# Position bias as a small relu layer, x transposed on TensorE, v loaded once, more buffers of p

## The chip, the cores and the metric

The kernel runs on one core of a Trainium2 chip. The metric is the device time of one execution in microseconds (us), lower is better. Engines are TensorE (PE; its weight loads are PEld), VectorE (DVE), ScalarE (ACT), GpSimd (POOL) and SyncE (SP), with 16 DMA engines beside them. SP and ACT issue DMAs from queues of their own.

## The reference

Attention with a bias that depends on positions, then two mixing blocks. B = 4 batches, H = 8 heads, S = 576 positions, D = 64, hidden layer of 32. In short:

```python
scores = q @ k.T / 8
x = log1p(abs(i - j)) / log1p(max(i, 1))          # S x S
bias = relu(x[..., None] @ w1 + b1) @ w2          # S x S x H, the same for all batches
attn = softmax(scores + bias)
x = (attn @ v), heads side by side                # B x S x 512
# block 1: h = gelu(x @ w_in); u, v = halves of h; layer norm of v; v_s = w_sg @ v + b_sg
x = x + (u * v_s) @ w_out
# block 2: theta = x @ w_theta; y = w_tok_r @ (x cos theta) + w_tok_i @ (x sin theta)
u = x + y;  out = u + relu(u @ w_ch)
```

## The kernel before

The program records every operation with its operands, and a planner in `Rec.plan` (a list scheduler) decides on the order in which each engine gets them. It has a price for every operation (`cost`), a due time (`nc.key`, moved by the table `SHIFT`), a choice of engine for operations with alternatives (`BIAS`), and knows when buffers come free. Buffers are taken from tags with a fixed number of copies, and the copies of one tag are handed out in the order of the program text. Every instruction is emitted from one helper line (L377), so groups are told apart by the names of their tiles.

The stages, in the order of the text of `build`:

- `bias_gen`. The bias for all heads is built in SBUF, in `bm[0..3]` (128 query rows each, 8 heads, 576 columns) and `bm[4]` (the last 64 rows, two heads on the two halves of the partitions). A relu unit is on where a distance lies above a threshold, so for 45 blocks VectorE compares a table of distances `ds` with thresholds `th` into `mk` (128x2048 f16, rows are 4 columns times 32 units), TensorE multiplies `mk` by `w2*w1` and by `w2*b1`, each in two f16 parts `ch` and `cl` (1440 products of 64 columns), ScalarE copies one half out (`cc`), VectorE multiplies the other by x (`bt`; for some blocks GpSimd does it from a copy `ca`), and GpSimd adds the two into the bias. Beside it ScalarE squares all of v (`vr`) for a scale.
- `att_pair`, for 4 batches and 4 pairs of heads. `prep` loads k and q (`kq`) and v (`raw`, 128x1152 f32: all of v's rows in nine blocks of 128, the list of rows being v twice) and makes f16 parts `v16`. A pair has nine tiles: four blocks of 128 queries for each head, and the last 64 queries of both heads in one tile. Per tile (`att_tile`): scores by f32 products, bias added and the row's extreme found in one VectorE operation (`e`), Exp on ScalarE, p in two f16 parts (the high one on ScalarE as a rule, the low one on GpSimd), one transposing DMA from SP's queue into `pT` (nine blocks of 128x128), and products of `pT` with `v16` into `px`, one PSUM tile that all pairs share.
- The pair's result is divided by the row sums (`pair_main`, `pair_rem`), cut into two f16 parts (`x16`), transposed by a DMA into `xp`, and stored in DRAM (`dx`).
- `mlp(b)`: the first half of block 1 for batch b. It loads `xT` from `dx` and runs 15 units of f16 products (`vp`, `up`, `sp`), each into a PSUM tile of tag `c` (three copies), and stores its result to `dg`. In the program text mlp(b) stands behind the pairs of batch b and ahead of those of b+1; its due time lies well inside batch b+1.
- The tail: conversion of f64 weights, `s2` (the second half of block 1, which reads x again from `dx` as `xx` and adds its two parts on GpSimd), `theta`, `ymix` and `s4` (block 2).

Of the kernel before, what the change touches and what calls it, by code (L numbers as in the profile page):

```python
# [26 lines left out]
NP = H // 2  # L27
# [32 lines left out]
class V:  # L60
# [3 lines left out]
    def __getitem__(self, idx):  # L64
# [3 lines left out]
        for k, n in enumerate(self.shape):  # L68
# [4 lines left out]
            if d is not None:  # L73
                o = box[d][0]
                box[d] = (o + lo, o + hi)
# [119 lines left out]
def lap(a, b):  # L195
    return all(x[0] < y[1] and y[0] < x[1] for x, y in zip(a, b))


def covers(a, b):
    return all(x[0] <= y[0] and y[1] <= x[1] for x, y in zip(a, b))  # L200
# [3 lines left out]
    ("bsg", "scalar"): -41.5201, ("bsg", "sync"): -39.1168, ("g", "scalar"): -6.4798, ("g", "sync"): -12.4768,  # L204
    ("gg", "gpsimd"): -53.3129, ("gg", "scalar"): 53.8735, ("gg", "sync"): -40.1577, ("gg", "vector"): 12.8746,
    ("gr", "scalar"): 40.0426, ("gr", "sync"): -7.2604, ("ident", "scalar"): 17.1516,
    ("ident", "sync"): 113.1953, ("kq", "scalar"): -21.5876, ("kq", "sync"): -29.2704, ("m", "gpsimd"): -0.0246,
    ("m", "vector"): -0.3984, ("n", "gpsimd"): 35.1559, ("n", "scalar"): -32.6866, ("n", "vector"): -2.2379,
    ("oo", "scalar"): -24.802, ("oo", "sync"): 41.6395, ("p", "gpsimd"): -12.0341, ("p", "scalar"): 0.77,
    ("p", "vector"): 2.7135, ("raw", "scalar"): -44.0014, ("raw", "sync"): 28.1704,  # L210
    ("raww_ch", "scalar"): -43.3259, ("raww_ch", "sync"): 25.28, ("raww_out", "scalar"): 10.1527,
    ("raww_out", "sync"): -7.508, ("raww_theta", "scalar"): -30.2437, ("raww_theta", "sync"): 36.9561,
    ("raww_tok", "scalar"): -80.3857, ("raww_tok", "sync"): -15.2151, ("rawwi", "scalar"): 13.2129,
    ("rawwi", "sync"): 14.8861, ("ri", "gpsimd"): -15.2269, ("ri", "vector"): 3.6268,
# [4 lines left out]
    ("wr_w_ch", "gpsimd"): 3.5242, ("wr_w_ch", "vector"): 6.6705, ("wr_w_out", "gpsimd"): 21.1998,  # L219
    ("wr_w_out", "vector"): -58.3817, ("wr_w_theta", "gpsimd"): -22.3734, ("wr_w_theta", "vector"): -49.8466,  # L220
    ("wr_w_tok", "gpsimd"): -17.5048, ("wr_w_tok", "vector"): -57.1214, ("ws", "scalar"): -34.0239,
    ("ws", "vector"): 34.9878, ("wsr", "scalar"): 49.7733, ("wsr", "vector"): 31.3292,
# [5 lines left out]
}  # L228
SHIFT = {
# [355 lines left out]


T0, TS = 88.0, 2.35
TWO = range(4,45,6)
PBN = (0,0,1)
T2 = T0 + TS * 144  # L590

# [761 lines left out]
```

## Time and profile before

| | before |
|---|---|
| runs, median (lowest to highest) | 920.55 us (917.52 to 922.99), 3 runs |
| the profiled execution: time | 922.0 us |
| the profiled execution: span from the first to the last instruction | 920.2 us |
| mean granted TensorE clock | 0.894 |
| busy: PE, DVE, ACT, POOL | 81%, 72%, 57%, 46% of the span |

Busy time is the time in which an engine has an instruction under way. Products overlap, so that a busy TensorE need not be at its peak. The granted clock is a share of 2.4 GHz. A group of instructions is named by what it writes and reads, as `pT<-p`; what ended an engine's idle time stands behind it with an arrow.

### The profile page before, as it was taken

Reading aid. Unit: us, or ns where it says so; the run is one execution under the profiler, and the core shown is the slowest. Engines: PE = TensorE matmul, PEld = TensorE weight load, DVE = VectorE, ACT = ScalarE, POOL = GpSimd, SP = SyncE. Lnnn points to the kernel's source line nnn. Section 1 sums busy time; section 2 is a strip of 40 time slices with the busy share of each in tenths; the row PEclk is TensorE's granted clock in tenths of the full one; section 3 lists DMA queues with packets and bytes.
Section 4 is the critical chain, followed back from the end, with each engine's and each line's share of the span. In section 5 each row is a group of like instructions: output and inputs, shape, how many; then the busy total and the mean of one; then the engine's idle time right before and its main releaser. Section 6 shows DMA issues by size and latency. Waiting matters only on the chain. (4 is left out here: it accounts for less than half of the span.)

```text
span 920.2 us, 19119 instructions
## 1 busy us (share of the span) xinstructions
PE 742.5 (81%) x7322; PEld 558.2 (61%) x7322; DVE 660.5 (72%) x1391; ACT 525.5 (57%) x1064; POOL 421.0 (46%) x363
## 2 busy tenths in 40 slices
PE   3555356757769878789897989999878999999998
PEld 3554343544544444455455545567767999989998
DVE  8989975799787865477764776989999782472712
ACT  6432247888777865567865764756666651261600
POOL 3777685555655645465654653333244521140400
PEclk9768776875788988899998899999889999999999
DMA  8300029999999999999899877355631100010001
GB/s 290 102 1 1 1 77 208 179 201 202 221 218 198 198 174 165 202 188 190 181 197 219 143 144 246 113 179 159 210 114 35 47 31 21 14 39 1 34 19 52
DMA packets 221307, 120.04 MB, mean 130 GB/s; under 512 B 195104, under 2 KB 195232, under 8 KB 221216
## 3 DMA queue, kind: packets, MB, share of 16 engines
q1 hardware_dynamic: 215360, 104.40, 51.7%
q10 hardware_dynamic: 5856, 14.42, 6.2%
q8 instruction: 57, 0.93, 0.4%
q14 instruction: 34, 0.28, 0.1%
HBM read 57.45 MB, written 14.16 MB: 78 GB/s over the span
## 5 line engine op out<-in xcount | busy, mean ns | idle before, releaser
L377 POOL TENSOR_TENSOR p<-e,p 128x576 f16<-128x576 f32 x144 | 189.1, 1322 | 127.7 <-ACT p L377 84.2
L377 PEld LDWEIGHTS <-pT 128*128 128x128 f16 (+1 forms) x2240 | 87.1, 108 | 114.3 <-DMA pT<-p 66.5
L377 PE MATMUL px<-v,pT 128*128 128x64 f16 (+1 forms) x2240 | 100.3, 204 | 64.8 <-DMA pT<-p 55.2
L377 PE MATMUL s<-kq 64*128 64x288 f32 (+1 forms) x640 | 138.1, 508 | 15.9 <-DVE m L377 10.1
L377 DVE CUSTOM_DVE_ANT_0 e<-s,bias 128x576 f32<-128x576 f32 x128 | 95.7, 752 | 62.6 <-PE s L377 47.6
L377 ACT ACTIVATE e<-e,m 128x576 f32<-128x576 f32 x144 | 110.2, 766 | 49.2 <-DVE m L377 35.4
L377 PE MATMUL yp<-wk,z 128*128 128x288 f32 x864 | 117.3, 296 | 0.0
L377 ACT ACTIVATE p<-e 128x576 f16<-128x576 f32 x142 | 94.1, 671 | 40.2 <-DMA pT<-p 38.0
L377 PEld LDWEIGHTS yp<-wk,z 128*128 128x128 f32 x864 | 115.3, 188 | 0.4
L377 PE MATMUL pb<-ch,mk 128*128 128x64 f16 x720 | 60.8, 214 | 58.2 <-ACT cc L377 33.9
L377 PEld LDWEIGHTS s<-kq 64*128 64x128 f32 (+1 forms) x640 | 71.4, 212 | 54.4 <-DVE m L377 22.1
L377 PEld LDWEIGHTS <-mk 128*128 128x128 f16 x1440 | 59.1, 112 | 60.6 <-DVE mk L377 46.0
L377 DVE TENSOR_TENSOR mk<-ds,th 128x2048 f16<-128x2048 f16 x45 | 80.4, 1831 | 5.4 <-PE pb L377 5.4
L377 POOL TENSOR_TENSOR bias<-bt,cc 128x512 f32<-128x512 f32 x36 | 63.6, 1789 | 34.3 <-ACT cc L377 34.3
L377 PE MATMUL op<-sp_g,wo 128*128 128x288 f32 x384 | 61.9, 320 | 14.1 <-DVE x L377 12.8
L377 PEld LDWEIGHTS op<-sp_g,wo 128*128 128x128 f32 x384 | 57.2, 206 | 19.0 <-issue 10.6
L377 ACT ACTIVATE cc<-pb,ci 128x512 f32<-128x512 f32 x45 | 29.5, 685 | 64.2 <-DVE bt L377 62.2
L377 PE MATMUL vp<-wi,xT 128*128 128x512 f16 (+1 forms) x240 | 64.9, 408 | 0.8 <-DMA xT<-dx 0.8
L377 PE MATMUL sp<-ws,n 128*128 128x64 f16 (+1 forms) x384 | 58.8, 293 | 3.6 <-DVE n L377 3.1
L377 PE MATMUL pb<-cl,mk 128*128 128x64 f16 x720 | 60.7, 214 | 0.0
L377 PE MATMUL up<-xT,wi 128*128 128x64 f16 (+1 forms) x384 | 57.8, 297 | 0.0
L377 DVE TENSOR_TENSOR x<-x,yp 128x576 f32<-128x576 f32 x16 | 12.0, 753 | 62.8 <-PE yp L377 62.8
(217 smaller groups left out, 1381.7 us busy)
## 6 DMA issues: line engine op xcount, KB each, us to landing
kq<-kq SPq DMA_DIRECT2D x13, 576.0 KB, 5.4
raw<-vp SPq DMA_DIRECT2D x10, 576.0 KB, 4.9
raww_tok<-w_tok SPq DMA_DIRECT2D x18, 288.0 KB, 3.1
vr<-v_all SPq DMA_DIRECT2D x12, 384.0 KB, 4.1
xx<-dx SPq DMA_DIRECT2D x16, 288.0 KB, 3.4
out<-oo SPq DMA_DIRECT2D x16, 288.0 KB, 2.1
gr<-dg SPq DMA_DIRECT2D x14, 288.0 KB, 3.3
dg<-gg SPq DMA_DIRECT2D x14, 256.0 KB, 3.0
```

What stands on the lines that cost most here:

```text
L377: getattr(getattr(self.nc, name), m)(*[res(x) for x in a], **out)
```

## The change

The bias: one hidden unit of one query row is relu(w1/psi_i * log1p|i-j| + b1). A table `lt` holds log1p of distances for 32 units times 4 rows that lie 8 apart; a window of it, times a per-partition `sl`, gives the hidden layer of four query rows as one 128x576 f32 tile `hq`. There are 36 groups G of four such tiles. Two groups of three make them on VectorE, as max(window*sl, -b1), to which a constant per head is added back at the end; every third on ScalarE, as Relu with scale and bias. Eight f32 products multiply them by w2 (128 rows to 32 outputs: 4 rows times 8 heads), with the four tiles of a group going to partitions 0, 32, 64 and 96 of the same PSUM tile. One evacuation makes `bs`, and a DMA copies its 128 rows to bias rows 8 apart (for the last 64 query rows four smaller DMAs). `mk`, `bt`, `cc`, `ca` and the tables for them go.

x: the pair's f32 result is transposed on TensorE (`flip`: four transposes of 128x128, and one of 64x128) into a PSUM tile of tag `c`, and both f16 parts are made from there into `xT`, which stays in SBUF (six copies, one per pair) and is stored to `dx` for the tail. mlp reads it in SBUF.

v: the first five blocks are loaded, and the other four are copied on VectorE between the two halves of the partitions. p16 has six copies instead of four, pT eight instead of four. The planner's constants (`BIAS`, `SHIFT`, yields, some prices) have other values throughout.

```diff
@@ bias_gen
-        for n in range(45):
...
-                nc.vector.tensor_tensor(mk, win, th[:, ib * P:(ib + 1) * P].bc(1, 16), op=ALU.is_gt)
...
-            for J in range(16):
...
-                nc.tensor.matmul(o, mk[:, J, :], chv, start=True, stop=False)
-                nc.tensor.matmul(o, mk[:, J, :], clv, start=False, stop=True)
...
-            nc.scalar.activation(cc, pv[:, H:], AF.Copy, scale=ci8)
...
-                self.tt(("gpsimd",), dv, tmp[r, :nh], cc[r, hs], ALU.add)
+        for G in range(36):
...
+            lut = G % LUTG == LUTG - 1
+            for q in range(4):
...
+                h = st.tile([P, S], F32, tag="hq", bufs=10, name=f"hq{Q}")
+                win = lt[:, DOFF - i0:DOFF - i0 + S]
+                if lut:
+                    nc.scalar.activation(h, win, AF.Relu, scale=sl[:, Q:Q + 1], bias=b1)
+                else:
+                    nc.vector.tensor_scalar(h, win, sl[:, Q:Q + 1], nb, op0=ALU.mult, op1=ALU.max)
+                hs.append(h)
+            for n in range(2):
+                for q in range(4):
+                    nc.tensor.matmul(ps[32 * q:32 * q + 32, n, :SH], w2f, hs[q][:, n * SH:(n + 1) * SH],
+                                     start=True, stop=True)
...
+            nc.any(("scalar", "activation", (bv, ps[:, :, :SH], AF.Identity), {"bias": add}),
+                   ("vector", "tensor_scalar", (bv, ps[:, :, :SH], add, None), {"op0": ALU.add}))
             if ib < 4:
+                self.ld(self.bm[ib][c:P:8], bs)
             else:
+                for k in range(2):
+                    for e in range(2):
+                        self.ld(self.bm[4][64 * e + c + k:64 * e + 64:8], bs[64 * k + e:64 * k + 64:2])
@@ prep
-        raw = a.tile([P, 2, S], F32, tag="raw", bufs=1, name=f"raw{u}")
+        raw = a.tile([P, 2, 5 * D], F32, tag="raw", bufs=1, name=f"raw{u}")
...
-        self.cp(v16[:, 0], vr, self.sv)
+        self.cp(v16[:, 0, :, 0:5], vr, self.sv)
+        nc.vector.tensor_copy(v16[0:64, 0, :, 5:9], v16[64:P, 0, :, 0:4])
+        nc.vector.tensor_copy(v16[64:P, 0, :, 5:9], v16[0:64, 0, :, 1:5])
@@ att_tile
-        p16 = a.tile([P, 2, S], F16, tag="p16", bufs=4, name=f"p{u}")
+        p16 = a.tile([P, 2, S], F16, tag="p16", bufs=6, name=f"p{u}")
-        pT = a.tile([P, 9, P], F16, tag="pT", bufs=4, name=f"pT{u}")
+        pT = a.tile([P, 9, P], F16, tag="pT", bufs=8, name=f"pT{u}")
@@ pair_main, pair_rem
-        self.cp(x16[:, :4, 0], xf)
-        self.tt(("gpsimd", "vector"), x16[:, :4, 1], xf, x16[:, :4, 0], ALU.subtract)
+        self.flip(p, u, xf, xT, 0, 4)
+
+    def flip(self, p, u, xf, xT, o, n):
+        nc = self.nc
+        m = xf.shape[0]
+        w = m * n
+        pt = self.cps(f"xq{u}")
+        for t in range(n):
+            nc.tensor.transpose(pt[:, t * m:(t + 1) * m], xf[:, t] if n > 1 else xf, self.ident[:m, :m])
+        self.cp(xT[:, 0, o:o + w], pt[:, :w])
+        nc.vector.tensor_tensor(xT[:, 1, o:o + w], pt[:, :w], xT[:, 0, o:o + w], op=ALU.subtract)
@@ att_pair
-        x16 = a.tile([P, 5, 2, P], F16, tag="x16", name=f"x16_{b}_{p}")
-        xp = a.tile([P, 2 * S], F16, tag="xp", bufs=1, name=f"xp{b}_{p}")
+        xT = self.xT[b, p] = self.p_x.tile([P, 2, S], F16, tag="xT", bufs=6, name=f"xT{b}_{p}")
...
-        nc.sync.dma_start_transpose(out=xp.rearrange("p (t k) -> p t k", k=P),
-                                    in_=x16.rearrange("p t s k -> p (t s k)")[:, 0:1152])
-        self.ld(self.dx[b, :, p], xp)
+        self.ld(self.dx[b, :, p], xT.rearrange("p s t -> p (s t)"))
@@ mlp
-        self.xT = self.p_x.tile([P, 4, 2 * S], F16, tag="xT", name=f"xT{b}")
-        for p in range(0, NP, 2):
-            self.ld(self.xT[:, p:p + 2], self.dx[b, :, p:p + 2])
@@ s2
+            nc.gpsimd.tensor_tensor(xs, xx[:, :S], xx[:, S:], op=ALU.add)
```

## Rows read from the trace of the kernel before

**Rows 1.** The page's head.

```profile
span 920.2 us, 19119 instructions
```

**Rows 2.** Three stages: us, busy us (instructions) by engine, granted clock, DMA, GB/s.

```profile
0.00:138.00 138.00, 68.35 (x1460) 63.11 (x1460) 118.08 (x147) 53.58 (x92) 91.36 (x68) 0.79 0.23 79
138.00:548.00 410.00, 328.79 (x3488) 195.64 (x3487) 296.19 (x811) 298.88 (x642) 225.44 (x204) 0.85 1.00 192
548.00:920.00 372.00, 345.32 (x2375) 299.48 (x2375) 246.27 (x434) 173.10 (x331) 104.19 (x92) 0.98 0.26 81
```

**Rows 3.** Groups of 0 to 134 us: busy us, mean ns, idle before.

```profile
L377 DVE TENSOR_TENSOR mk<-ds,th 128x2048 f16<-128x2048 f16 x45 | 80.4, 1831 | 5.4 <-PE pb L377 5.4
L377 POOL TENSOR_TENSOR bias<-bt,cc 128x512 f32<-128x512 f32 x36 | 63.6, 1789 | 34.3 <-ACT cc L377 34.3
L377 PE MATMUL pb<-ch,mk 128*128 128x64 f16 x720 | 60.8, 214 | 58.2 <-ACT cc L377 33.9 <-DVE mk L377 18.8 <-DVE bt L377 5.5
...
L377 ACT ACTIVATE cc<-pb,ci 128x512 f32<-128x512 f32 x45 | 29.5, 685 | 64.2 <-DVE bt L377 62.2 <-PE pb L377 1.7
```

**Rows 4.** SP's queue from 515 us: start, us, what it issued.

```profile
524.85 14.72 SPq L377 DMA_TRANSPOSE pT<-p  x8
```

**Rows 5.** DMA issues: count, KB each, median us to landing.

```profile
xT<-dx ACTq DMA_DIRECT2D x5, 576.0 KB, 6.7
...
pT<-p SPq DMA_TRANSPOSE x144, 4.0
...
xp<-x SPq DMA_TRANSPOSE x16, 4.2
```

**Rows 6.** Waits of the engines, whole span: us in total, times, longest.

```profile
PEld L377 <- DMA pT<-p: 66.5, 36, 5.6
...
PE px L377 <- DMA pT<-p: 55.2, 30, 5.0
...
ACT p L377 <- DMA pT<-p: 38.0, 16, 5.2
```

**Rows 7.** Waits of SP's queue, 138 to 548 us.

```profile
SPq L377 <- POOL p L377: 103.9, 73, 4.2
```

**Rows 8.** The table prow in the start: ns min/median/max, first and last start.

```profile
L377 DVE TENSOR_SCALAR prow<-prow,rt x1: 520/520/520, 6.4 to 6.4; 128x576 f32<-128x576 f32 x1
L377 DVE TENSOR_SCALAR prow<-prow x1: 460/460/460, 7.0 to 7.0; 128x576 f32<-128x576 f32 x1
```

**Rows 9.** The tile xt.

```profile
L377 ACT ACTIVATE xt<-xt,ci x5: 758/774/777, 8.9 to 11.9; 128x576 f32<-128x576 f32 x5
```

**Rows 10.** The tile vr.

```profile
L377 ACT ACTIVATE vr<-vr x12: 827/843/844, 6.5 to 35.9; 128x768 f32<-128x768 f32 x12
```

**Rows 11.** The PSUM tile xp of the tail.

```profile
L377 DVE TENSOR_TENSOR rk<-xp,rk x18: 672/684/692, 676.1 to 872.8; 128x512 f32<-128x512 f32 x16, 64x512 f32<-64x512 f32 x2
```

**Rows 12.** TensorE in order of time, at 220 and at 313 us.

```profile
220.25 2.85 PE L377 MATMUL s<-kq 64*128 64x288 f32 x8
...
313.39 1.24 PE L377 MATMUL s<-kq 64*128 64x288 f32 x8
314.57 0.58 PE L377 MATMUL px<-v,pT 128*128 128x64 f16 x14
```

**Rows 13.** The tile s of the scores.

```profile
L377 PE MATMUL s<-kq x640: 402/403/846, 126.8 to 533.3; 64*128 64x288 f32 x128, 64*64 64x288 f32 x32
```

**Rows 14.** The chain that ended last: start, us, what.

```profile
756.79 0.66 PE xp L377 x4
```

**Rows 15.** The tile v.

```profile
L377 ACT ACTIVATE v<-raw,fc_v x16: 1238/1248/1256, 129.3 to 511.6; 128x1152 f16<-128x1152 f32 x16
```

**Rows 16.** The page's costliest groups: the products of the MLP.

```profile
L377 PE MATMUL vp<-wi,xT 128*128 128x512 f16 (+1 forms) x240 | 64.9, 408 | 0.8 <-DMA xT<-dx 0.8
...
L377 PE MATMUL sp<-ws,n 128*128 128x64 f16 (+1 forms) x384 | 58.8, 293 | 3.6 <-DVE n L377 3.1
...
L377 PE MATMUL up<-xT,wi 128*128 128x64 f16 (+1 forms) x384 | 57.8, 297 | 0.0
```

More of the change, by code (lines that the diff above doesn't have):

```diff
@@ L195, in lap @@
 def lap(a, b):
-    return all(x[0] < y[1] and y[0] < x[1] for x, y in zip(a, b))
+    return all(x[0] < y[1] and y[0] < x[1] and not (x[2:] and x[2:] == y[2:] and (x[0] - y[0]) % x[2])
+               for x, y in zip(a, b))
 def covers(a, b):
-    return all(x[0] <= y[0] and y[1] <= x[1] for x, y in zip(a, b))
+    return all(x == y or (not x[2:] and x[0] <= y[0] and y[1] <= x[1]) for x, y in zip(a, b))
 BIAS = {
-    ("bsg", "scalar"): -41.5201, ("bsg", "sync"): -39.1168, ("g", "scalar"): -6.4798, ("g", "sync"): -12.4768,
@@ L205 @@
[L205 to L209, printed above, removed]
@@ L587 @@
 T0, TS = 88.0, 2.35
-TWO = range(4,45,6)
-PBN = (0,0,1)
+LUTG = 3
 T2 = T0 + TS * 144
@@ L704, in bias_gen @@
-        self.th = nc.vector.tensor_scalar(th, y2, 0.5, sg2, op0=ALU.add, op1=ALU.mult)
-        nc.vector.tensor_scalar(ds, ds, sg2, None, op0=ALU.mult)
-        c32 = st.tile([P, 2, H, 4], F32, name="c32")
-        nc.vector.memset(c32, 0.0)
+        sl = st.tile([P, S // 4], F32, name="sl")
+        lt = st.tile([P, DW], F32, name="lt")
+        for x, n in ((wb, "wb"), (sl, "rpsi"), (lt, "ltab")):
+            self.ld(x, d[n])
+        nb = st.tile([P, 1], F32, name="nb")
+        nc.vector.tensor_scalar(nb, b1, -1.0, None, op0=ALU.mult)
@@ L708, in bias_gen @@
+        self.th = nc.vector.tensor_scalar(sl, sl, w1, None, op0=ALU.mult)
+        w2s = st.tile([P, 4, H], F32, name="w2s")
+        nc.vector.memset(w2s, 0.0)
         for g in range(4):
             r = slice(32 * g, 32 * g + 32)
-            nc.vector.tensor_scalar(c32[r, 0, :, g], w2[r], w1[r], None, op0=ALU.mult)
-            nc.vector.tensor_scalar(c32[r, 1, :, g], w2[r], b1[r], None, op0=ALU.mult)
-        c32f = c32.rearrange("p a h g -> p (a h g)")
-        junk = self.bsg[:, :64]
-        for i in range(2):
-            nc.scalar.activation(junk, c32f, AF.Square, accum_out=self.ss_c[:, i:i + 1])
@@ L725, in bias_gen @@
-        for n in range(45):
-            nc.key = 2.0 * n
-            ib, js = divmod(n, 9)
-            if js == 0:
-                nc.any(("scalar", "activation", (xt[:, ib], xt[:, ib], AF.Copy), {"scale": ci8}),
-                       ("vector", "tensor_scalar", (xt[:, ib], xt[:, ib], ci8, None), {"op0": ALU.mult}))
-            mk = st.tile([P, 16, P], F16, tag="mk", bufs=3, name=f"mk{ib}_{js}")
-            off = DOFF + ib * P - js * 64
+            nc.vector.tensor_scalar(w2s[r, g], w2[r], 8.0, None, op0=ALU.mult)
@@ new lines, in bias_gen @@
+        w2f = w2s.rearrange("p g h -> p (g h)")
+        cb = st.tile([P, 1], F32, name="cb")
+        bb = st.tile([P, 1], F32, name="bb")
+        pc = self.ps_b.tile([P, 2, 512], F32, tag="pb", bufs=2, name="pbc")[:, 0]
+        nc.vector.tensor_copy(bb, b1)
+        for g in range(4):
+            nc.tensor.matmul(pc[32 * g:32 * g + 32, 0:1], w2f, bb, start=True, stop=True)
+        nc.vector.tensor_copy(cb, pc[:, 0:1])
+        zero = st.tile([P, 1], F32, name="zb")
+        nc.vector.memset(zero, 0.0)
@@ L1308, in layout @@
     a["wb"] = np.tile(w, (4, 1))
-    pos = np.arange(S)
-    pi = np.log1p(np.maximum(pos.astype(f), f(1.0)))
-    a["prow"] = np.tile(pi[None], (P, 1))
-    a["dtab"] = np.abs(np.arange(DW)[None] - DOFF - (np.arange(P) // HID)[:, None]).astype(np.float16)
-    rel = np.log1p(np.abs((pos[:, None] - pos[None]).astype(f)))
-    x = (rel / pi[:, None]).astype(f)
-    x = np.concatenate([x, x[512:]], axis=0)
-    a["xtab"] = x.reshape(5, P, S).transpose(1, 0, 2)
+    psi = np.log1p(np.maximum(np.arange(S).astype(f), f(1.0)))
+    rows = [[G // 8 * P + G % 8 + 32 * q if G < 32 else 512 + 2 * (G - 32) + 32 * (q % 2) + q // 2 for q in range(4)]
+            for G in range(36)]
+    rows = np.array(rows).reshape(1, S // 4) + 8 * np.arange(4)[:, None]
+    a["rpsi"] = np.repeat(f(1.0) / psi[rows], HID, axis=0)
+    a["ltab"] = np.log1p(np.abs(np.arange(DW)[None] - DOFF - 8 * (np.arange(P) // HID)[:, None]).astype(f))
     a["ident"] = np.eye(P, dtype=f)
```

188 lines of the change are left out of this document (65 added, 123 removed), and 33 rows, old and new, of tables (BIAS, SHIFT).

## Prediction

> **What bounds the kernel now.** I read the page's head and its 40 slices first, then busy time by stage, then each stage's own groups, prices, queue and waits. The profiled execution has a span of 920.2 us and a time of 922.0; the median of the runs shown is 920.55, so what holds for the profile holds for the median less 1.5 us [rows 1]. Cut at the first transposing DMA of p (138 us) and behind the last products with p (548 us), the kernel has three stages [rows 2]. In the start (138 us) the DMA engines work 0.23 of the time, and VectorE 118 of 138 us. In the attention (410 us) no engine is above 329 of 410, but the DMA share is 1.00. In the tail (372 us) TensorE is busy 345 us at a granted clock of 0.98, and the chain that ended last lies there, on its matmuls.
>
> The start makes the bias. VectorE's 45 comparisons that write mk take 80 us, GpSimd's adds into bias 64, TensorE's two products with mk 61 each, and TensorE waits for mk and for cc [rows 3]. It is a cycle of four engines at VectorE's pace.
>
> In the attention each tile's p goes through one transposing DMA. Eight of them issued back to back by SP take 14.72 us, 1.84 each, where nothing but the DMA engines holds the queue [rows 4]. 160 of them (144 of p, 16 of x; a tile of 128x1152 f16, 0.295 MB) [rows 5] make 294 us of the 410. The rest, 116 us, is for ordinary copies: 192 GB/s times 410 us [rows 2] is 78.7 MB, less 160 x 0.295 MB, so 31.5 MB at 3.7 us per MB. TensorE and ScalarE wait for pT: 66.5 us before weight loads, 55.2 before products, 38.0 before p is written [rows 6]. Against a pure DMA bound speaks in the same stretch that SP itself waits 103.9 us for GpSimd's half of p [rows 7]: the producers are not far ahead.
>
> **The start, part by part.** Removed: mk, the 1440 products, bt, cc and GpSimd's adds. Added: 144 relu tiles of 128x576 f32, 96 on VectorE and 48 on ScalarE (every third group of four rows' tiles); 288 f32 products of 288 columns with 32 rows of output; 36 evacuations; 48 copies of bias rows (10.6 MB).
> - VectorE: a 128x576 tensor_scalar takes 0.46 us with constants and 0.52 with one per-partition operand [rows 8]; the new one has two. Lower bound 0.52, upper one step of 0.06 more; I take 0.58: 96 x 0.58 = 56 us.
> - ScalarE: 0.774 with one per-partition operand [rows 9]; two, by a like step, 0.87: 48 x 0.87 = 42 us. The 12 squares of v stay, 0.84 each [rows 10], 10 us.
> - Evacuations go to either engine: cc's 128x512 took 0.685 on ScalarE [rows 3], an operation reading 128x512 from PSUM 0.684 on VectorE [rows 11]; for 576 columns about 0.76: 36 x 0.76 = 27 us.
> - Sum 135 us on two engines, 68 each if shared evenly. Work starts at about 9 us (before, the first products start at 11), so the relu work ends at 77; the first transpose of p came 4 us behind the first attention tile, and I add 2 for uneven sharing: 83 us instead of 138, **-55**.
> - TensorE must stay under those 68 us. An f32 product of 288 columns is two passes, and the scores show eight passes, two at a time on the two halves of the rows, in 1.24 us at full clock [rows 12], each recorded as 0.40 to its end [rows 13]. Four steps with the last one whole: (1.24 - 0.40)/3 = 0.28 a step, the first with its weight load in it; I take 0.25, a product 0.50. 288 products, four side by side, are 36 us; two by two 72; one after another 144. Side by side in columns is not in this trace, only in rows; the scores overlap fully, so I take 36 to 72, hidden behind the 68 or nearly. The Trainium skill (TensorE: Matmul & The Clock Gate, Part 3: packing small matmuls) gives 2.38 times for three column tiles; by that 58 us, an estimate, also hidden.
> - Copies: the start now moves 138 us x 79 GB/s = 10.9 MB [rows 2]; with 10.6 more and 1.5 of table less, 20 MB at 3.7 us per MB is 74 us, under the 83. The cover is thin: at 4.2 us per MB the copies would set the end. The 3.7 was measured beside the transposes, which the start has none of, so I leave the copies at nothing; at twice the price they would add 65.
>
> **The attention.** The 16 transposes of x go: 16 x 1.84 = 29 us of DMA. v is read as 640 f32 columns instead of 1152, 256 KB less each, 15 times in this stage (3.9 MB), and the reads of xT for three batches go, 6 x 576 KB (3.5 MB) [rows 5]: 7.4 MB x 3.7 = 27 us. So the DMA work falls by 56, from 410 to 354. The Trainium skill (Advanced Engine Details and Errata, X-Bar Transpose) expects 350 to 400 GB/s of a transposing DMA; one of 295 KB would take 0.8 us, an estimate, the 16 be worth 13, and the fall be 40. The eight in 14.72 us contradict it.
>
> What takes the place: TensorE gets five small transposes per pair; four f32 ones of 128x128 take 0.66 us [rows 14], so with the fifth about 0.9, 14 us in all, and its 329 become 343 at the clock then granted. VectorE has x's subtraction now from PSUM, 0.68 by the nearest row [rows 11], where it was from SBUF, and gets two copies of 64x512 f16 per pair, bounded by the 0.46 above and by nothing: 0 to 15 us on 296. ScalarE converts 640 instead of 1152 columns, 1.248 us now [rows 15], about 7 us less in all. None reaches 354, but all stand at 83 to 97% of it.
>
> There is also a new order. The flip's PSUM block comes from the tag that the MLP uses, three buffers handed out in the program's order, and mlp(b) stands ahead of the pairs of batch b+1. So flip(b+1, 0) waits until mlp(b) is nearly through; xf and xfr have one buffer each, so the next pair's px can't be emptied, and attention stops some 16 tiles into batch b+1. Behind it wait the products with p, then pT (8 buffers), then SP's transposes. mlp(b) needs 65, 58 and 59 us by four [rows 16], 45 us of TensorE. The 16 tiles need half of 1.24 for scores and at most 0.58 for px each [rows 12], 19 us. Together 64, against (16 + 8) x 354/144 = 59 us of cover. Lower bound of the price nothing; upper bound, with the MLP alone in all three batches but for the eight buffered tiles, 3 x (45 - 20) = 75. The need is nearest to the cover, so I take a stall of 5 per batch and some refilling, 20 us in all: 354 + 20 = 374, **-36**. p and pT with 6 and 8 buffers I cost at nothing by themselves; they are in this cover.
>
> **The tail.** x's way through DRAM to the last mlp goes, but TensorE is busy 345 of 372 us there [rows 2]: **-3**, between 0 and -15 where mlp(2) moves ahead of the attention's end. xs by one GpSimd add instead of two is off the path. The planner's other constants only reorder; I give them no sign.
>
> **Sum.** 922.0 - 55 - 36 - 3 = 828 by the profile's time, 827 by the median.
>
> **Rivals.**
> 1. *The attention keeps its length.* SP's 104 us of waiting for GpSimd speak for it, and the new order; the waits for pT against. 922 - 55 - 3 = 864, with the upper bound of the stall (354 + 75 = 429) 883.
> 2. *Column groups don't overlap, at full clock.* 144 us of products instead of 68: start 9 + 144 + 6 = 159, +21; 922 + 21 - 36 - 3 = 904. For it only that the trace has no such case.
> 3. *Slower than before.* The same, at the lower level of the clock. The start's granted clock is 0.79 now [rows 2], between the levels of 1.2 and 2.4 GHz; at the lower one the eight passes took 2.85 us instead of 1.24 [rows 12], so a product is 1.0. Start 9 + 288 + 6 = 303, +165: 1048. It decides once a product costs more than (138 + 39 - 15)/288 = 0.56 us, a price between those of the two levels. Against it: in the tail, where TensorE has hardly a gap, 0.98 was granted [rows 2].
> 4. *All of the DMA's relief shows, and mlp(2) leaves the tail.* 922 - 55 - 56 - 15 = 796.
>
> **Chances.** Forecast 0.55, with its own range 805 to 850; rival 1 0.22; rival 2 0.07; rival 3 0.05; rival 4 0.09; a change that nets out to nothing 0.02. The range 785 to 890 takes in rival 4, rival 1 with its bound, and leaves out rivals 2 and 3 and a little. A measurement of this kernel tells about 0.5% from no change: faster 0.93, same 0.02, slower 0.05.
>
> **What the profile after would show.** The first transpose of p at 75 to 95 us; VectorE and ScalarE both above 0.8 in the start; four hq products starting within a few tens of ns of each other (if 0.24 us apart, rivals 2 or 3); 144 transposes, none of x; attention of 355 to 390 us with waits for pT shorter, and stalls, if any, where a batch begins, with the flip's block behind the MLP. I am wrong if the start is bound by the copies or TensorE, or if p is late at GpSimd as often as before.

## The result, and the profile after

| | before | after |
|---|---|---|
| median (lowest to highest) | 921.77 us (917.52 to 927.09), 4 runs | 884.49 us (881.56 to 889.14), 4 runs |
| profiled execution: time, span | 922.0, 920.2 us | 881.6, 879.8 us |
| mean granted TensorE clock | 0.894 | 0.917 |

The ratio is 0.960 [0.953, 0.967]: 37 us faster. The forecast's sum had 94 us. More than half of that gain did not come, and the rest of this text is about where it went.

The page of the changed kernel, its head, its busy times and three of its rows of 40 slices:

```profile
span 879.8 us, 17586 instructions
...
PE 762.3 (87%) x6544; PEld 534.8 (61%) x6544; DVE 629.9 (72%) x1475; ACT 520.5 (59%) x1038; POOL 298.4 (34%) x263
...
PE   5689778648899889997999976998878999999998
...
PEclk9979956557999999999799996999999999999999
DMA  7987689729898299866998396465622210010101
```

The head answers to [rows 1]. TensorE is busier than before (762 us against 742) in a shorter span, the DMA engines are no longer full in the middle, and the clock row has one hole, in slices 6 to 10 (110 to 220 us).

For the stages, the first cut of [rows 2] (the first transpose of p) no longer parts anything, since the first pair's attention now runs beside the bias: its first transpose is issued at 53 us. So both kernels are cut at the tenth transpose of p (the second pair's first tile) and at the end of the products with p. Columns as in [rows 2]. Before:

```profile
0.00:164.00 164.00, 85.84 (x1602) 73.13 (x1603) 132.98 (x193) 72.85 (x143) 105.14 (x81) 0.78 0.36 99
164.00:549.00 385.00, 311.83 (x3360) 186.14 (x3358) 281.28 (x765) 279.60 (x591) 211.66 (x190) 0.86 1.00 191
549.00:920.00 371.00, 344.80 (x2369) 298.96 (x2366) 246.27 (x434) 173.10 (x331) 104.19 (x92) 0.98 0.26 82
```

After:

```profile
0.00:119.00 119.00, 90.21 (x747) 40.83 (x748) 81.64 (x192) 82.12 (x137) 16.35 (x20) 0.90 0.81 190
119.00:536.00 417.00, 349.40 (x3620) 207.19 (x3620) 309.73 (x860) 271.45 (x580) 215.76 (x184) 0.87 0.79 158
536.00:880.00 344.00, 322.64 (x2183) 286.73 (x2180) 238.49 (x423) 166.94 (x322) 66.25 (x60) 0.97 0.25 79
```

Start -45, attention **+32**, tail **-27**; the forecast had -55, -36 and -3. In the attention the DMA share fell from 1.00 to 0.79 and the stage still got longer. TensorE is busy 38 us more there and 22 less in the tail: the third MLP, which before ran in part after the attention, is now done inside it (its last product at 508 us, before at 568).

**The start.** Groups that answer to [rows 3]: busy us, mean ns, idle before.

```profile
L379 PE MATMUL pb<-hq,w2s 128*32 128x288 f32 x576 | 69.3, 454 | 14.3 <-DVE bs L379 9.9 <-ACT hq L379 2.2 <-DVE hq L379 1.6
L379 DVE TENSOR_SCALAR hq<-lt,sl,nb 128x576 f32<-128x576 f32 x96 | 49.8, 586 | 2.4 <-PE pb L379 1.6 <-DMA lt<-ltab 0.7
L379 ACT ACTIVATE hq<-lt,wb,sl 128x576 f32<-128x576 f32 x48 | 38.8, 859 | 3.5 <-DVE m L379 2.1 <-PE s L379 0.8 <-issue 0.5
```

The prices are those of the forecast (0.59 us for 0.58, 0.86 for 0.87), yet the last bias product starts at 101 us, where the forecast had the relu work end at 77. Two windows of the start, columns as above:

```profile
10.00:55.00 45.00, 33.52 (x300) 13.79 (x300) 35.17 (x65) 34.59 (x56) 1.96 (x3) 0.92 0.89 202
55.00:101.00 46.00, 43.96 (x318) 18.95 (x318) 35.26 (x82) 33.03 (x50) 4.97 (x5) 0.93 0.69 152
```

No engine that makes hq is full. Up to 55 us the DMA engines are at 0.89, at 0.89 x 45 us for 202 GB/s x 45 us = 9.1 MB, 4.4 us per MB; the forecast had 3.7 and said that at 4.2 the copies would set the end. That they did is not shown: between 10 and 55 us VectorE waits 5.6 us for the copies of `bs`, ScalarE 7.1 us for the reads of `vr`, and TensorE 9.9 us for VectorE's `bs`. From 55 us on TensorE is at 0.96. In order of time on TensorE (start, us, what):

```profile
29.93 1.18 PE L379 MATMUL pb<-hq,w2s 128*32 128x288 f32 x16 [1.83 <-DVE bs L379]
...
69.72 4.64 PE L379 MATMUL pb<-hq,w2s 128*32 128x288 f32 x41
```

Where all four tiles of a group are there, its 16 passes take 1.18 us: less the last one's 0.40, 0.78 for three more steps of four, 0.26 each, so four column groups do run side by side. At 70 us 41 passes take 4.64: (4.64 - 0.40)/40 = 0.106 each, 2.5 side by side; products start there with the first tile of a group.

**The attention.** Waits that answer to [rows 6]: us in total, times, longest.

```profile
PEld L379 <- DMA pT<-p: 28.6, 18, 4.9
...
ACT p L379 <- DMA pT<-p: 22.2, 12, 4.1
PE px L379 <- DMA pT<-p: 21.9, 15, 4.1
```

They are 0.4 to 0.6 of before [rows 6], shorter as forecast. SP's own wait for GpSimd's half of p, the warning of [rows 7], is 73.6 us in 57 waits, where the same cut of before has 90.9 in 67:

```profile
SPq L379 <- POOL p L379: 73.6, 57, 3.7
```

Instead attention halts. SP's queue, the transposes of p alone (start, us from the start of the first issue to the end of the last, count):

```profile
137.94 9.48 SPq L379 DMA_TRANSPOSE pT<-p  x6
...
167.51 1.32 SPq L379 DMA_TRANSPOSE pT<-p  x1
198.49 16.58 SPq L379 DMA_TRANSPOSE pT<-p  x8
...
275.07 5.78 SPq L379 DMA_TRANSPOSE pT<-p  x3
302.39 2.06 SPq L379 DMA_TRANSPOSE pT<-p  x1
308.15 23.71 SPq L379 DMA_TRANSPOSE pT<-p  x12
```

None is issued between 169 and 198, and none between 281 and 302. TensorE at the end of the second halt:

```profile
296.30 2.00 PE L379 MATMUL up<-xT,wi 128*128 128x512 f16 x50
298.13 1.68 PE L379 MATMUL sp<-ws,n 128*128 128x512 f16 x7
299.94 0.27 PE L379 MATMUL xq<-ident,xfr 64*128 64x64 f32 x1
300.14 1.04 PE L379 MATMUL sp<-ws,n 128*128 128x512 f16 x4
301.75 0.57 PE L379 MATMUL px<-v,pT 128*128 128x64 f16 x14 [0.58 <-DVE xfr L379]
```

The MLP of batch 0 is at its last units; only then comes the flip `xq`, behind it px, and with px the transposes. It is the order that the forecast described, and near the place it named: 25 tiles of a batch are transposed, where it had 16 whose products are done and eight more in the buffers. From tile 18 to tile 27 of a batch (counted from 0), which takes in the halt, it is 51, 44, 39 and 38 us in the four batches, where it was 22 to 27 before. Batch 0's halt has another cause, since no MLP is under way there. The tile `xq` (duration min/median/max in ns, first and last start in us):

```profile
L379 PE MATMUL xq<-ident,xf x64: 272/273/476, 167.0 to 537.9; 128*128 128x128 f32 x64
L379 DVE CAST xT<-xq x32: 206/432/692, 205.4 to 538.4; 128x512 f16<-128x512 f32 x16, 128x64 f16<-128x64 f32 x16
```

The first flip runs at 167 us, and the cast that empties its block comes at 205, behind the last piece of `wi` (201 us). In the code the pool of xT is opened after `w1_load` has released its staging pool, so the first xT has no memory until the weights are converted; xf, px and the transposes stand behind it.

### The profile page after: what moved, and what is told of

It is laid out like the page before. It is cut to its first block, busy times and chain, and to the rows that moved or that the text cites. A ratio compares the mean times of both kernels' runs of the same rounds, so it can differ in the third digit from the quotient of the medians.

```text
span 879.8 us, 17586 instructions
## 1 busy us (share of the span) xinstructions
PE 762.3 (87%) x6544; PEld 534.8 (61%) x6544; DVE 629.9 (72%) x1475; ACT 520.5 (59%) x1038; POOL 298.4 (34%) x263
## 4 chain that ended last, share of the span: by engine, by line
PE 52%; DVE 17%; DMA 15%; issue 7%; ACT 5%; POOL 3%; SPq 1%; ACTq 0%; DVEq 0%; POOLq 0%
PE yp L379 12%; PE s L379 8%; PE cp L379 6%; DMA pT<-p 6%; PE pb L379 6%; PE sp L379 5%; PE tp L379 4%; PE up L379 4%; PE px L379 4%; PE vp L379 3%; POOL p L379 2%; DVE v L379 2%; DMA vr<-v_all 2%; DVE e L379 2%; DVE cvaw_tok L379 2%
## 5 line engine op out<-in xcount | busy, mean ns | idle before, releaser
L379 PE MATMUL s<-kq 64*128 64x288 f32 (+1 forms) x640 | 149.1, 495 | 21.5 <-DVE m L379 21.5
L379 PE MATMUL px<-v,pT 128*128 128x64 f16 (+1 forms) x2240 | 95.4, 204 | 32.6 <-DMA pT<-p 21.9
L379 PE MATMUL pb<-hq,w2s 128*32 128x288 f32 x576 | 69.3, 454 | 14.3 <-DVE bs L379 9.9
L379 PEld LDWEIGHTS op<-sp_g,wo 128*128 128x128 f32 x384 | 54.4, 194 | 12.4 <-DVE x L379 4.9
L379 PEld LDWEIGHTS pb<-hq,w2s 128*32 128x32 f32 x576 | 28.4, 117 | 52.9 <-DVE bs L379 9.9
L379 ACT ACTIVATE sp_u<-x 128x576 fp32r<-128x576 f32 x16 | 10.8, 684 | 70.8 <-DVE x L379 70.1
L379 PE MATMUL cp<-sp_u,wc 128*128 128x288 f32 x384 | 52.5, 295 | 0.0
L379 PE MATMUL tp<-wt,sp_t 128*128 128x512 f32 x192 | 47.9, 403 | 4.3 <-DVE sp_t L379 2.6
L379 DVE TENSOR_SCALAR hq<-lt,sl,nb 128x576 f32<-128x576 f32 x96 | 49.8, 586 | 2.4 <-PE pb L379 1.6
L379 PEld LDWEIGHTS cp<-sp_u,wc 128*128 128x128 f32 x384 | 51.2, 188 | 0.2
```

Source lines behind the costliest of these rows:

```text
L379: getattr(getattr(self.nc, name), m)(*[res(x) for x in a], **out)
```

## The experiments

Theories. **A**: the order of the shared PSUM blocks (tag `c`) causes the halts, and the halts ate the gain. **B**: TensorE's work, or its idle time, sets the total; the halts only move MLP work from the tail into the attention. **C**: the planner's new constants carry the gain. **D**: w_in's conversion, which gets its staging memory only when the bias is done, holds back batch 0 and all behind it. The forecast's own theory is that DMA work sets the attention's length.

Two scales stand below. The ratio compares a run with the kernel before, measured beside it (medians of 914 to 918 us); the time in us stands by itself. Against the changed kernel, whose own kernel before took 922, a run's ratio makes it 3 to 13 us slower than its time does.

**The shared block alone** (A against B). Three runs: the flip in a block of its own, its control, and the MLP's text interleaved with the pairs.

```diff
# e1_own_block
-        pt = self.cps(f"xq{u}")
+        pt = self.ps_c.tile([P, 512], F32, tag="xq", bufs=1, name=f"xq{u}")
# e1_own_block and e1c_two_blocks
-        return self.ps_c.tile([P, 512], F32, tag="c", bufs=3, name=u)
+        return self.ps_c.tile([P, 512], F32, tag="c", bufs=2, name=u)
# e2_interleave (pT 6 and xT 8 buffers; mlp returns run)
+                if b:
+                    run(4 * p, 4 * p + 4)
```

> After the change the attention halts four times, once in batch 0 and once in each later batch, with 39 to 51 us for nine tiles instead of some 21. Theory A (order): the flips' PSUM block comes from the MLP's tag, so they stand behind w1_load's sums in batch 0 and behind the whole MLP of the batch before in the others. Here the flips have a tag of their own with one block, and the MLP keeps two. A expects the first flip at 120 to 145 us instead of 167, nine tiles never above 32 us, the last transpose of p at 490 to 515 us instead of 528, and a time of 845 to 872 us. Theory B (TensorE): with the DMA engines at 0.73 to 0.83, TensorE, busy 90 to 95% of batches 1 to 3, is what sets the pace, and the halts are only where the MLP's share is paid. B expects the halts to be spread out and the end of the attention and the time within 1% of 884.

> The other half of the run before: the shared tag with two blocks instead of three, flips still in it. A expects the halts to stay, at the same places or longer, and 880 to 905 us. B expects 884 to 900 as well, since the MLP alone loses a block. If it is as fast as the run with the own block, the own block is not what counts.

> The MLP's text of batch b is cut into four pieces of four units, and each stands behind a pair of batch b+1, so that the blocks of the shared tag are handed out in turn. xT has eight buffers for it, and pT six instead of eight, to make room. A expects the halts of batches 1 to 3 to go (nine tiles in 20 to 30 us each), that of batch 0 to stay, and 850 to 875 us. B expects 876 to 892.

Measured, ratio to before: own block 894.6 us, 0.979 [0.974, 0.984]; control 926.3 us, 1.012 [1.006, 1.018]; interleaved 905.1 us, 0.987 [0.983, 0.992]. At the place of the first halts the theory holds: tiles 18 to 27 of batches 1 to 3 take 22, 20 and 18 us with the own block (interleaved 24, 24 and 22; control 57, 51 and 55). Batch 0's halt stays (63 us): the first flip now runs at 129 us, but the first cast to xT at 202, when the weights are done. The own block's tile `xq`:

```profile
L379 PE MATMUL xq<-ident,xf x64: 272/273/473, 129.2 to 535.9; 128*128 128x128 f32 x64
L379 DVE CAST xT<-xq x32: 197/442/693, 202.4 to 536.3; 128x512 f16<-128x512 f32 x16, 128x64 f16<-128x64 f32 x16
```

But two halts have only moved, to the ninth tile of the batches behind. SP's queue with the own block, the transposes of p alone:

```profile
324.41 10.12 SPq L379 DMA_TRANSPOSE pT<-p  x5
...
349.25 7.44 SPq L379 DMA_TRANSPOSE pT<-p  x4
...
418.72 6.77 SPq L379 DMA_TRANSPOSE pT<-p  x4
...
449.77 7.92 SPq L379 DMA_TRANSPOSE pT<-p  x4
```

The casts to xT that end them start at 346.2 and 446.8 us, as the last `up` products of an MLP, which read xT, are done. xT has six copies and the MLP's batch holds four, so the flip now waits for a copy of xT. Gaps of over 12 us between two transposes sum to 84 us in three, against 92 in four in the changed kernel. The own block's attention and tail:

```profile
117.00:516.00 399.00, 335.78 (x3436) 194.33 (x3436) 292.01 (x840) 269.66 (x574) 208.83 (x179) 0.85 0.83 160
516.00:893.00 377.00, 343.31 (x2364) 298.04 (x2362) 244.86 (x444) 170.72 (x328) 67.24 (x65) 0.96 0.25 77
```

The attention ends 20 us earlier than in the changed kernel and the tail is 33 longer: MLP work that the halts had taken in is back in the tail. Against its control, which has two blocks for the MLP and the flips together (attention 461, tail 350), the own block is 32 us faster, so halts can cost time. The interleaved run, with eight copies of xT, has no gap above 14 us behind batch 0, and still an attention of 422 us:

```profile
117.00:539.00 422.00, 342.11 (x3419) 202.72 (x3419) 290.98 (x838) 268.04 (x572) 206.43 (x177) 0.83 0.79 151
```

A names the cause of the halts in batches 1 to 3. That they ate the gain is not borne out, and not refuted either: the own block leaves the MLP two blocks and keeps halts, and the interleaved run has six buffers of pT.

**The start alone.** All eight products of a group wait for all four tiles, so that they always run four side by side.

```diff
+                    for x in ho:
+                        nc.dep(o, x)
```

> In the start TensorE's products of hq come as soon as one hq is there, so that most steps have two column groups side by side and not four; the sixteen passes of a group take 1.45 us and more, and TensorE is busy 44 of the 46 us before the bias is done at 101 us. Here the eight products of a group wait for all its four hq. Theory S (TensorE's order in the start): steps of four, 1.0 to 1.1 us a group, bias done at 88 to 95 us, time 870 to 880. Rival theory (copies): the bias copies and the reads of v, with the DMA share at 0.89 from 10 to 55 us, set the start; then the bias is done at 98 to 104 us and the time stays within 0.7% of 884.

886.4 us, 0.968 [0.964, 0.972]. The products' busy time falls and the bias ends at 94 instead of 101 us:

```profile
L379 PE MATMUL pb<-hq,w2s 128*32 128x288 f32 x576 | 58.1, 461 | 20.3 <-DVE bs L379 14.2 <-DVE hq L379 3.7 <-ACT bs L379 1.6
```

The seven us are not in the total: the attention's last product ends at 536 in both.

**One part undone at a time.** x through the transposing DMA and DRAM, as before; v read whole (pT with seven buffers for room); p and pT with four buffers; the bias as before. Each takes its function's text from the kernel before; the planner's constants stay those of the changed kernel. The diffs are those of the change, turned round.

> The changed kernel with x as before: two f16 parts transposed by a DMA, stored, and read back for each MLP; bias, v and buffers stay changed. The prediction's sum counts this part as 29 us of transposes and 13 us of reads of xT, less the 20 us of stalls that the flips' block was to cost: if DMA work still sets the attention's length, the time is 22 to 42 us above the changed kernel's 884, so 906 to 926. If TensorE sets the total (theory B), the attention has room for this DMA work (share 0.7 to 0.85 of 410 us) and TensorE loses 14 us of flips: 870 to 890.

> The changed kernel with v read whole (1152 columns instead of 640) and no copies between the halves of the partitions; pT has seven buffers instead of eight for room. The prediction's sum gives this part 3.9 MB at 3.7 us, so 14 us: 898 if DMA work sets the attention. If TensorE sets the total: 884, give or take 8 for another order of the planner's.

> The changed kernel with p and pT at four buffers each again. The prediction gave the buffers nothing by themselves, but counted the eight buffered tiles into the cover of the halts behind the MLP: without them each of three batches could halt some 8 us longer, at most 24 in all, so 884 to 908. If TensorE sets the total and is fed from the MLP while attention halts: 884, give or take 8, with a longer attention and a shorter tail.

> The changed kernel with the bias made as before (comparisons, f16 products, GpSimd's adds). The prediction's sum: 55 us above, 939. If what counts is where the start's gain was given back later (first attention 45 us earlier, end of the attention only 13 to 15 us earlier), then 13 to 30 us above, 897 to 914, and the first transpose of p at 130 to 140 us.

- x: 876.6 us, 0.964 [0.957, 0.972]. Nothing lost, where the forecast's sum had 22 to 42.
- v: 901.3 us, 0.990 [0.982, 0.998].
- buffers: 919.8 us, 1.009 [1.004, 1.013].
- bias: 948.9 us, 1.043 [1.035, 1.050]; the tenth transpose of p comes at 177 instead of 119 us, and the attention ends 58 us later too (594). In the kernel before the tenth transpose came at 164, so some 13 of the 58 may come from constants that were not made for the old bias.

The undone parts sum to far more than 37 us, so they do not add. The run with x by DMA is the telling one. Its attention and tail, and SP's queue at the place of the second halt:

```profile
116.00:502.00 386.00, 330.08 (x3340) 192.23 (x3341) 280.72 (x775) 275.59 (x600) 231.19 (x208) 0.85 0.98 187
502.00:875.00 373.00, 348.26 (x2380) 301.18 (x2378) 255.38 (x447) 174.95 (x334) 78.20 (x83) 0.97 0.25 81
```

```profile
273.03 20.44 SPq L379 DMA_TRANSPOSE pT<-p  x10
297.63 2.37 SPq L379 DMA_TRANSPOSE xp<-x  x1
300.06 1.70 SPq L379 DMA_TRANSPOSE pT<-p  x1
304.44 10.83 SPq L379 DMA_TRANSPOSE pT<-p  x6
```

No halt, the DMA share back at 0.98, an attention of 386 us, as long as before's 385, a tail of 373, as before's 371, and the same total as the changed kernel. So the flip, with its halts, leaves the total as it is: it trades 31 us of attention for 29 us of tail.

**Constants and due times** (C, D). The constants of the kernel before, and w_in's and w_sg's conversion due 48 units earlier.

```diff
# e5_w1_early
-        t = T0
+        t = T0 - 48.0
```

> The changed kernel with the planner's constants (engine choices, shifts of due times, load and yield factors) of the kernel before. Theory C: the new constants carry the gain, and with the old ones most of the 37 us go: 905 to 925. If the constants only reorder (as the prediction had it): 884, give or take 10.

> The changed kernel with the conversion of w_in and w_sg due 48 units earlier, inside the start, where VectorE and ScalarE have gaps, so that its sums in the shared PSUM tag are done before batch 0's first flip. If batch 0's halt (51 us for nine tiles at 101 to 220 us) costs time: it goes to about 25 us, and the time falls by 10 to 25 us to 860 to 875. If TensorE sets the total whatever the halt: 884, give or take 8; if the start gets longer by the conversion, up to 900.

Old constants (with no entries for the new tiles): 911.0 us, 0.997 [0.993, 1.001]. That is what C expected, but the second run warns: with nothing but other due times it takes 915.0 us, 1.004 [0.998, 1.009], above every range that was expected for it. And the conversion hardly moved: w_in's first load is issued at 102 us instead of 106, because its staging memory, by the code, is free only when the bias's is. So due times alone can cost 30 us.

**How far apart neighbouring plans lie, and D by itself.** Two runs with the same work and due times a hair different; one with the arithmetic of w_in's conversion left out; and the buffers alone, on the kernel before.

```diff
# n1_step_236
-T0, TS = 88.0, 2.35
+T0, TS = 88.0, 2.36
# n2_start_89
+T0, TS = 89.0, 2.35
# h1_no_conversion
-                self.conv64(sp, ri[:, cc, cs], src, 256, f"wi{half}_{k}")
...
+                self.cp(ri[:, cc, cs], raw[:, :, 1].bitcast(F32))
# b2_before_buffers, on the kernel before (p16, pT)
-bufs=4
+bufs=6
```

> The changed kernel with the due times of the attention's tiles 2.36 instead of 2.35 units apart: the same work, a slightly other plan. If plans close to this one cost the same: 880 to 890, and the 20 to 35 us that the undone parts and the doses cost are theirs. If the changed kernel's plan is a lucky one among its neighbours: 895 to 915, and of each of the earlier runs that amount is the plan's and not the edit's.

> As the run before, by another way: the attention's due times begin at 89 instead of 88 units. 880 to 890 if neighbouring plans cost the same, 895 to 915 if the changed kernel's plan is a lucky one.

> The changed kernel with the arithmetic that turns w_in from f64 into f32 left out: its 16 pieces are loaded as before, and the high words go on as they are, by one copy instead of seven operations. Theory D: the weights' conversion, which gets its staging memory only when the bias is done (101 us) and ends near 200, holds back batch 0 and the first MLP, and TensorE idles at a low clock meanwhile: then w_in is ready near 160, the first MLP's products begin 30 to 50 us earlier than 218, and the time falls by 20 to 45 us, to 840 to 865. If batch 0's stretch costs nothing that the tail would not take anyway: 875 to 890.

> The kernel before with six buffers of p and six of pT instead of four (there is no room for eight) and nothing else. The prediction gave the buffers nothing by themselves. Undone alone in the changed kernel they cost 35 us. If they are worth that by themselves: 890 to 905. If the kernel before is bound by DMA work and the four suffice, or if a kernel's own plan is always better than its neighbours: 915 to 935.

The neighbours take 880.1 us, 0.958 [0.954, 0.963], and 883.4 us, 0.963 [0.959, 0.968]: a small disturbance costs nothing, a larger one (e5) up to 30 us. Without the conversion's arithmetic: 881.7 us, 0.962 [0.956, 0.968]. The last w_in sum comes at 167 instead of 196 us, batch 0's nine tiles take 36 us instead of 51, the first MLP starts at 193 instead of 218, the attention ends 14 us earlier, and nothing is left of it at the end:

```profile
118.00:522.00 404.00, 347.61 (x3615) 205.48 (x3614) 287.63 (x815) 256.41 (x539) 201.82 (x167) 0.89 0.82 161
522.00:879.00 357.00, 327.88 (x2183) 290.50 (x2180) 242.05 (x423) 166.41 (x322) 68.28 (x60) 0.96 0.24 76
```

D holds for about half of batch 0's halt (x by DMA has 22 us there) and falls as the cause of the missing gain. The buffers on the kernel before: 926.1 us, 1.011 [1.007, 1.015]; alone they bring nothing there.

**Work added and taken away** (B against the forecast's DMA). Added: scores of two blocks of each pair computed twice; 24 tiles of p transposed twice. Taken away: the products of p with v's low part; four ninths of each transpose of p (the products that would read those blocks read others again).

```diff
# d1_pe_dose
-        for n in range(2):
+        for n in [0, 1] * (1 + (t in (0, 2))):
# d2_dma_dose (pT 7 buffers)
+        if kind == 0 and (t == 0 or (t == 2 and p % 2 == 0)):
+            pd = a.tile([P, 9, P], F16, tag="pd", bufs=1, name=f"pd{u}")
+            nc.sync.dma_start_transpose(out=pd, in_=p16.rearrange("p s j -> p (s j)"))
# m1_less_pe
-            seq = [(c, 0) for c in range(9)] + [(c, 1) for c in range(5)]
+            for c in range(9):
+                nc.tensor.matmul(o, pT[:, c, cs], v[:, 0, e, c], start=c == 0, stop=c == 8)
# m2_less_dma
+        nc.sync.dma_start_transpose(out=pT[:, 0:5], in_=p16.rearrange("p s j -> p (s j)")[:, 0:640])
```

> The changed kernel with more TensorE work in the attention and nothing else: the scores of two of the four blocks of each pair are computed twice into the same PSUM tile, 32 times eight passes. At 1.24 us by eight passes at full clock that is 40 us, at the lower level more. If TensorE sets the total (theory B): 30 to 45 us above the changed kernel, 915 to 930. If halts in the order or DMA set it: 884 to 895.

> The changed kernel with more DMA work in the attention and nothing else: 24 of the 144 tiles of p are transposed a second time, into a tile that nobody reads; pT has seven buffers for room. 24 times 1.84 is 44 us. If DMA still sets the attention: 915 to 930. If TensorE sets the total (theory B): 884 to 892, with the DMA share of the attention up by about 0.1.

> The changed kernel without the products of p with the low part of v: 5 of the 14 products of a tile's block are left out, everything else stays. At 0.58 us for 14 at full clock that is 33 us of TensorE in the attention (160 blocks of 14). If TensorE's work sets the total (theory B): 850 to 860. If DMA work or the order of the shared PSUM blocks sets it: 876 to 890.

> The changed kernel with less DMA work in the attention: only the first 640 of the 1152 columns of a p tile are transposed, and the products that would read the other four blocks read the first ones again, so TensorE's work is the same and the low part of p is left out. 4/9 of 144 times 1.84 us is 118 us of DMA work. If DMA still sets the attention, as the forecast had it: 800 to 840. If TensorE sets the total: 870 to 885, with the attention's DMA share near 0.5 and the attention's end up to 20 us earlier.

More TensorE work: 915.5 us, 1.004 [0.998, 1.010], 31 above the changed kernel by the times and 40 by the ratios, for a dose of 40. More DMA work: 904.5 us, 0.995 [0.990, 1.000], 20 or 33 above for a dose of 44, between what the two theories expected. Less TensorE work: 892.4 us, 0.975 [0.966, 0.985]. Less DMA work: 897.0 us, 0.982 [0.973, 0.990]. Neither that takes away is faster. The attention with four ninths of p's transposes left out:

```profile
118.00:544.00 426.00, 365.80 (x3619) 212.11 (x3616) 308.62 (x863) 270.96 (x581) 214.06 (x184) 0.85 0.55 112
```

118 us of DMA work are gone, the share is 0.55, and the stage takes 426 us instead of 417. In the changed kernel DMA work does not set its length, and this is more than any plan's 30 us could hide. Where the time went can be seen: tiles 18 to 27 take 208 us instead of 173, the rest of the stage 218 instead of 244. What the transposes gave back, the halts took. B in the form "the time follows TensorE's work" did not pass either: the products with p are busy 25 us less (70.7 us against 95.4), and the time is 8 us longer.

**One sum over all.** Every span is TensorE's work at full clock, plus what the lower clock adds, plus its idle time. Work is busy time times granted clock, summed over windows of 20 us; "nine tiles" is the sum over the four batches of tiles 18 to 27, which misses the two halts that moved with the own block.

| kernel | span | attention, tail | nine tiles | work | lower clock | idle |
|---|---|---|---|---|---|---|
| before | 920 | 385, 371 | 97 | 676 | 66 | 178 |
| after | 880 | 417, 344 | 173 | 711 | 51 | 118 |
| x by DMA | 875 | 386, 373 | 91 | 708 | 59 | 108 |
| neighbour n1 | 879 | 419, 343 | 172 | 713 | 50 | 116 |
| no conversion | 879 | 404, 357 | 160 | 710 | 53 | 116 |
| own block | 893 | 399, 377 | 123 | 714 | 54 | 124 |
| w1 early | 914 | 447, 353 | 196 | 721 | 61 | 132 |
| buffers 4 | 918 | 448, 342 | 196 | 715 | 67 | 136 |
| old bias | 946 | 417, 352 | 181 | 696 | 85 | 164 |
| more TensorE | 919 | 435, 353 | 205 | 748 | 54 | 117 |
| less TensorE | 893 | 430, 347 | 197 | 690 | 63 | 141 |
| less DMA | 898 | 426, 354 | 208 | 717 | 65 | 116 |

The six below "after" that do the same products agree in the column of work within 11 us (710 to 721), and the dose of 40 reads as 37. The column is a measure and no price: x by DMA lacks the flips, which the forecast put at 14 us, and reads 3 less. From before to after the 40 us are +35 work, -15 lower clock, -60 idle. By the rows of the stages, TensorE's idle time is 78, 73 and 26 us before, and 29, 68 and 21 after: 49 of the 60 are the start's.

## Why the prediction was wrong

**The start, -55: right mechanism, size off.** -45 at the tenth transpose, and 58 where the bias alone is undone, some 13 of which need not be the bias's own. VectorE's and ScalarE's prices held, products do run four side by side, and the four-engine cycle of [rows 3] is gone. What was mis-sized is the end of the bias, 101 us for 77. Products at 2.5 side by side are 7 us of that: making them four brought the end to 94, and the total nothing, so this term is not where the gain was lost. The copies at 4.4 us per MB may be part of the rest, which no run shows. (The sum's estimate from three column tiles is 144/2.38 = 60 us, not 58; nothing hangs on it.) That the first pair's attention would run inside the start was not foreseen: first transpose at 53 us, forecast 75 to 95. It lies beside the bias, whose end came 24 us late, so that the term came out near its size is in part luck.

**The attention, -36: the step that failed.** It reads "the DMA work falls by 56, from 410 to 354", and takes that as the stage's length. The fall is real (0.79 x 417 us = 329 us of DMA work, and the waits for pT are shorter), but the length did not follow: 385 became 417. The DMA share of 1.00 in [rows 2] was taken for the bound. In the changed kernel it is none: with 118 us of transposes left out the stage is no shorter, and with x's 16 transposes and the reads of xT back it is shorter, at the same total. Of the kernel before it is shown only that 1.00 was no ceiling. With six buffers of p and pT its attention took 370 us, at a share of 1.06 and with a tail of 398:

```profile
163.00:533.00 370.00, 307.96 (x3310) 185.14 (x3308) 272.25 (x747) 271.35 (x578) 211.75 (x183) 0.86 1.06 200
```

There is another reading, in which the relief came and the halts ate it: tiles 18 to 27 take 76 us more than before, the rest of the stage 44 less (244 for 288), and the sum is +32. The runs do not separate it. With the own block, which keeps 84 us of halts, the rest takes 276; interleaved, almost without halts behind batch 0, it takes some 300. So the 44 are at least in part what the buffers catch up behind a halt.

**The stall of 20 us: right place, size off.** Tiles 18 to 27 take 173 us in the four batches against 91 with x by DMA. In batches 1 to 3, the only ones that the step counted, it is 52 more, where it had 20 in all with an upper bound of 75. Batch 0, with 29 more, was left out: there xT waits for the weights' staging memory, and TensorE's granted clock is 0.59, mostly the lower level of 1.2 GHz. Rows of after:

```profile
119.00:220.00 101.00, 68.15 (x555) 42.49 (x554) 75.96 (x228) 70.83 (x178) 46.41 (x43) 0.59 0.75 160
220.00:536.00 316.00, 281.25 (x3069) 164.70 (x3066) 233.77 (x633) 200.62 (x403) 169.34 (x141) 0.96 0.80 157
```

and of before, at the same tiles:

```profile
164.00:243.00 79.00, 52.02 (x566) 35.79 (x563) 66.62 (x181) 64.12 (x155) 45.81 (x40) 0.74 0.99 197
243.00:549.00 306.00, 259.80 (x2794) 150.35 (x2795) 214.66 (x584) 215.48 (x437) 165.86 (x150) 0.90 1.00 190
```

22 of the 32 us of lengthening lie in batch 0; behind it TensorE does 21 us more in 10 us more.

**The tail, -3: -27.** The forecast gave mlp(2)'s move at most 15. It moves because of the halts: while attention stands, TensorE runs the MLP.

**Together.** The second and third errors are one. Attention and MLP share TensorE, so where MLP work takes the place, a stall of the attention costs little and an earlier end of it gains little: own block (-20 and +33), no conversion (-13 and +13), x by DMA (-31 and +29). It does not always: the control with two blocks has 44 us more of attention than the changed kernel and 6 more of tail. The forecast added up stages that trade work with each other. What remained is the start's gain, which is nearly the whole result: -45 of -40, with +32 and -27 behind it. Rival 1, "the attention keeps its length", at 864, came nearest in the number. By its parts that is luck: the attention grew and the tail shrank, and it had neither. Of its two reasons the new order is shown to halt the attention; a late GpSimd was not tested.

**The buffers, "nothing by themselves": so on the kernel before, not here.** There six and six brought nothing; in the changed kernel four cost 35 us. Tiles 18 to 27 take 196 us instead of 173 with four, so most of the attention's 31 us more lies where the forecast had put it, in the cover of the halts.

**What stays open.** Why the plans differ: e5 shows that due times alone are worth 30 us, so the differences of that size (v whole, old constants, more DMA, less TensorE) can't be put down to the edit. Where flips stay in the shared tag, slower plans have longer halts (173 us and a span of 880, 196 and 914 to 918), but less TensorE work (197 and 893) and less DMA work (208 and 898) fit no rule. A flip that waits for nothing of the MLP's, with all three blocks left to the MLP, more copies of xT and eight buffers of pT, was not tried; it would decide whether the halts cost the missing gain. Nor was GpSimd's half of p taken away, for which SP's queue waits 73.6 us after the change and 105 with x by DMA. No version that was run is faster than the changed kernel beyond its interval.

## What to carry to other kernels

A share of 1.00 tells that a resource is loaded; that the stage is bound by it shows only when the stage moves with that work; before relying on it, ask who would be late next and whether work from another stage will fill the gap. Where two stages share an engine and a planner may move work between them, forecast them together, by that engine's work, its idle time and its clock, instead of adding a change for each. And a buffer put into a tag that another stage uses takes that stage's place in the order: its price is the cover that other buffers still give. When a halt is gone from its place, look through the whole trace for it: here the next tag with too few copies made it again, half a batch later.

## What the runs showed of the hardware that was not expected

- f32 products with 32 rows of output, four to the four column groups, cost one step of 0.26 us for four passes; the scores' two at a time took 0.28 [rows 12, 13]. The Trainium skill (TensorE: Matmul & The Clock Gate, Part 3) gives 2.38 times for three column tiles; the trace agrees that column tiles overlap, here four of them: 16 passes in 1.18 us.
- Copies of 2304-byte rows between SBUF partitions, beside the reads of v, cost 4.4 us per MB with hardly a transpose among them; the whole middle stage of before, mostly transposes, moved its ordinary copies at an estimated 3.7.
- TensorE without products that had kept it busy for 25 us was busy only 10 us less (752.5 against 762.3): its mean granted clock fell from 0.917 to 0.898, and its idle time rose from 118 to 141 us.
